# Attention and a cosine-gated MLP on one core: the weights' low-word bits taken by ScalarE from one byte, the word's shift folded into the join, and the gate's cosine as one sine

## The chip, the cores and the metric

The kernel runs on one core of one Trainium2 chip. The time is device microseconds of that core, from three executions of the kernel before: 662.24 us as their median, 661.46 and 663.5 us at the ends. The profile is of one more execution, taken by the hardware profiler.

## What is computed

Two stages. The first is attention over 4 batches, 8 heads, 768 positions and head size 64: each position sees its neighbours within 15 positions and, beside them, 24 summaries (the maximum of the keys and the mean of the values of each block of 32 positions). The second is an MLP on the 3072 resulting rows of 512 numbers, with a gate that multiplies by a cosine:

```python
x = np.ascontiguousarray(attn_out.transpose(0, 2, 1, 3)).reshape(B * S, H * D)
h = x @ w_in                 # 3072x512 @ 512x2048
g = h * np.cos(h)
return (g @ w_out).astype(np.float32)
```

The two weight matrices arrive as 64-bit floating-point numbers. The kernel has no 64-bit arithmetic, so it reads them as pairs of 32-bit integer words and puts a 32-bit number together from each pair.

## The kernel before

**Attention** is cut into 32 groups: 8 blocks of 384 rows, times 4 pairs of heads called a, b, c, d. A group's steps are transposes of queries and keys, score products, a maximum, a subtraction on POOL, an exponential on ACT, sums, a multiplication by their inverse on POOL, transposes of the weights of attention, and the product with the values, which leaves 128 columns of x, again as a high and a low part.

**The MLP** is cut into 128 *steps* s0 to s127, each of one block of 384 rows and one of 16 slices of 128 hidden units. Its products are done in a format with fewer mantissa bits, so every operand is split into a high part and a low part, and each product is three products. A step has *up* (12 matrix products, L714), then the gate, a chain on one tile t: *turns* (ACT, L724, h over 2 pi, rounded by the conversion to an integer), *residue* (DVE, L727, h minus 2 pi times the turns), *sine* (ACT, L732, of half the residue), *square* (ACT, L735, times 2), *gate* (DVE, L739, minus 1 and times h). Since cos h is 1 minus twice the squared sine of h/2, t then holds minus h cos h; the sign is put right when the result is taken from PSUM. Then *high_part* (a CAST to gh on ACT or DVE), *low_part* (gl), and 9 products with the second weights, L770: 6 with gh, 3 with gl. The steps run in the order block 0 slices 0 to 5, block 1 slices 0 to 15, block 0 slices 6 to 15, then the other blocks, 16 slices each.

**The weights' slices** w0 to w15 are converted in the first quarter of the program, each just ahead of the first step that uses it. A slice is 128x1024 pairs of words in one of the *late* buffers, and its steps are:

- *magnitude* (`ab`, ACT, L388): the high word read as a 32-bit float, made positive, into one of two *stage* buffers, `stage0` or `stage1`, each with room for one tile;
- *clamp* (`cl`, DVE or POOL, L393), in place;
- *shift* (`sh`, DVE, L399): the word shifted left by 3 and its two top bits masked off, from the stage buffer into two PSUM banks;
- *last_bits* (`lb`, DVE, L407), called the join from here on: the low word shifted right by 29, or-ed to it, in PSUM;
- *first_bits* (`fb`, DVE, L415): the high word's two top bits or-ed to it, from PSUM into a stage buffer;
- *high_part* and *low_part* (`hi`, L350 or L352; `lo`, L356): the slice's tile w.

**The order** is written out by hand. A string of tokens (`w3.sh.4.5` is slice 3's shift into banks 4 and 5; `s0.tu` is step 0's turns) is walked from the first to the last, each token issues its instructions, and every engine keeps its own instructions in that order. No scheduler moves them. Semaphores only make an engine wait where data or a buffer is not ready. So an instruction at the head of an engine's queue that waits holds back all that stand behind it there. The stage buffers add waits of their own: the magnitude of a slice can't write its stage buffer before the last reader of what lies there is done. In the kernel before that reader is the previous slice's shift; of a slice whose first_bits wrote into a stage buffer it is the low part.

The attention of blocks 0 and 1, the conversion of the slices, and the first MLP steps are interleaved in the first 95 us; after that most of the work is MLP steps, with the other blocks' attention between them.

Of the kernel before, what the change touches and what calls it, by code (L numbers as in the profile page):

```python
# [10 lines left out]
F32 = mybir.dt.float32  # L11
F32R = mybir.dt.float32r
I32 = mybir.dt.int32
AF = mybir.ActivationFunctionType
ALU = mybir.AluOpType
# [27 lines left out]
w8.sh.0.1 w3.hi.a b1.su a1.va.5 d1.z.0.v s1.tu c1.tp.0.7 w8.lb w3.lo.p a2.v d1.z.1.a c1.tp.1.3 s0.sq a2.tq.6 s1.re  # L43
c1.cp.1.a a1.xh.a s2.up.3 d1.mx s1.si c1.cp.0.a s0.ga d1.su w7.l w8.fb.0 s0.hi.a s1.sq c1.va.2 s0.lo.p w9.ab.1 s1.ga
w6.l s3.up.7 w8.hi.v s2.tu b2.q s1.hi.v d1.ex w9.cl.v s1.lo.p a1.xl s0.dh.0.1.4 s2.re w8.lo.p c1.xh.v s3.tu s0.dl
c1.xl s2.si s3.re s4.up.5 a2.cq.v v1_0.s.p d1.sm s2.sq s3.si s2.ga s1.dh w7.ab.0 d1.iv s2.hi.v d1.nm v1_1.l w9.sh.2.3
s1.dl s3.sq b1.ex s3.ga s2.lo.p d1.tp.0.6 w9.lb d1.tp.1.7 s2.dh w7.cl.p s4.tu b1.sm d1.cp.1.a s2.dl d1.cp.0.a s4.re
b1.iv s3.hi.a d1.va.7 w9.fb.1 b1.nm s4.si s5.up.6 w7.sh.2.3 s3.lo.p s4.sq w9.hi.v d1.xh.a s3.dh s4.ga s5.tu w9.lo.p
w10.ab.0 d1.xl s5.re s3.dl w7.lb s4.hi.a b1.tp.0.5 s5.si v1_1.s.p b1.tp.1.7 s4.dh b1.cp.1.a w7.fb.1 s5.sq b1.cp.0.a
s5.ga w7.hi.a b1.va.7 v1_2.l s4.lo.v w10.cl.v s4.dl s5.hi.a w7.lo.p b1.xh.a s5.dh b1.xl w10.sh.2.3 s6.up.5 v1_2.s.p  # L50
w6.ab.1 w10.lb s7.up.6 w10.fb.0 s6.tu s5.lo.p v1_3.l s6.re w12.l w6.cl.v s6.si s5.dl s7.tu w10.hi.v s8.up.7 s6.sq
s7.re w10.lo.p s5.ta.2.a s6.ga s7.si v1_3.s.v s7.sq s9.up.2 s5.ta.1.a s7.ga v1_4.l s6.hi.a w6.sh.4.5 s5.st.2 s5.ta.0.a
s6.lo.p b2.m s7.hi.a s10.up.3 s8.tu w6.lb s7.lo.p w12.ab.0 s8.re v1_4.s.p s11.up.6 w6.fb.1 s8.si s8.sq s9.tu s8.ga
v1_5.l w6.hi.a w12.cl.v s6.dh.4.5.7 w11.l s9.re w6.lo.p w12.sh.0.1 s9.si a2.m s6.dl s8.hi.a s7.dh s9.sq s5.st.1 s9.ga
s8.lo.p s5.st.0 w12.lb s7.dl s8.dh v1_5.s.p s10.tu s9.hi.a s10.re w12.fb.1 s10.si s8.dl s10.sq s12.up.2 v1_6.l
# [128 lines left out]
def tile_kernel(  # L184
# [20 lines left out]
    nc = tc.nc  # L205
# [156 lines left out]
    class Slice:  # L362
# [31 lines left out]

        def shift(self, *where):
            to = self.work_in(where)
            nc.vector.tensor_scalar(  # L399
                out=to, in0=self.u, scalar1=3, scalar2=0x3FFFFFFF,  # L400
# [557 lines left out]
```

## Time and profile before

| | |
|---|---|
| median of three executions | 662.24 us (661.46 to 663.5) |
| profiled execution, its span | 660.1 us |
| median less that span | 2.1 us |
| mean granted TensorE clock | 0.987 |
| HBM read, written | 53.72 MB, 15.73 MB |
| ACT table loads for the sine | 23, 29.5 us busy |

The profile counts, for each engine, the time in which an instruction ran. PE is the matrix engine's products and PEld its weight loads, which overlap them; DVE, ACT and POOL work on tiles; SP issues DMAs. A row of the groups' view gives line, engine, operation, output and input, shape and count, then the busy time in us and the mean of one in ns, then the engine's idle time just before these instructions and what ended most of it. A row of the timeline gives start and duration in us; a number after x is how many instructions the row joins, and square brackets hold the idle time ahead of it and the instruction or transfer that ended it. A row of the windows gives a stretch of the span and the busy time of each engine in it, then the granted clock, the DMA share and the rate.

### The profile page before, as it was taken

How to read it: one execution, taken by the hardware profiler on the slowest of the kernel's cores; microseconds unless marked ns; L12 is line 12 of the kernel's file. 1: busy time of each engine (PE TensorE's matmuls, PEld its weight loads, DVE VectorE, ACT ScalarE, POOL GpSimd, SP SyncE). 2: the span in 40 equal slices, each digit the busy share in tenths (PEclk: the TensorE clock that was granted, in tenths of full speed). 3: DMA queues.
4: the chain of work that ended last, by engine and by line, in shares of the span. 5: the costliest groups of instructions: out<-in, count | busy, mean ns of one | idle time of the engine just before them, and what ended most of it. 6: DMA issues, size and time to landing. Idle time of an engine off the chain costs nothing.

```text
span 660.1 us, 13282 instructions
## 1 busy us (share of the span) xinstructions
PE 632.6 (96%) x5141; PEld 560.2 (85%) x5141; DVE 449.7 (68%) x798; ACT 363.9 (55%) x640; POOL 221.8 (34%) x219
## 2 busy tenths in 40 slices
PE   6478999999999999999999999999999999999996
PEld 5256889989988998898898899889889989899985
DVE  4887999887855576668797777576876756433344
ACT  2656977776554485437477464356554645444342
POOL 4784896764430342301323411112330212010110
PEclk9869999999999999999999999999999999999999
DMA  9997906544243244525445433424364332000001
GB/s 224 259 271 203 276 15 223 169 109 71 55 122 85 91 124 132 127 59 114 111 107 135 147 98 97 114 43 85 115 163 104 92 94 70 5 1 17 16 17 48
DMA packets 167158, 72.68 MB, mean 110 GB/s; under 512 B 136824, under 2 KB 155832, under 8 KB 167096
## 3 DMA queue, kind: packets, MB, share of 16 engines
q1 hardware_dynamic: 167096, 71.84, 40.9%
q8 instruction: 40, 0.66, 0.4%
q14 instruction: 22, 0.18, 0.1%
HBM read 53.72 MB, written 15.73 MB: 105 GB/s over the span
## 4 chain that ended last, share of the span: by engine, by line
PE 86%; DMA 5%; SPq 3%; POOL 2%; DVE 1%; issue 1%; ACT 1%; DVEq 0%; POOLq 0%; ACTq 0%
PE banks L770 39%; PE banks L714 39%; PE banks L569 4%; PE banks L670 3%; DMA late<-in_moe_w_out_dram 3%; DMA late<-in_v_dram 1%; SPq L456 1%; POOL w L356 1%; DMA late<-in_q_dram 1%; POOL gl L356 1%; SPq L493 1%; POOL stage L393 0%; ACT stage L388 0%; PE banks L556 0%; DVE m L588 0%
## 5 line engine op out<-in xcount | busy, mean ns | idle before, releaser
L714 PE MATMUL banks<-xh,w 128*128 128x384 f32 x1024 | 272.1, 337 | 0.1
L770 PE MATMUL banks<-w,gh 128*128 128x512 f32 x768 | 198.1, 393 | 0.2 <-ACT gh L350 0.2
L714 PEld LDWEIGHTS banks<-xh,w 128*128 128x128 f32 x1024 | 185.9, 188 | 2.8 <-ACT pt L350 0.4
L714 PE MATMUL banks<-xl,w 128*128 128x384 f32 x512 | 171.4, 335 | 0.0
L770 PEld LDWEIGHTS banks<-w,gh 128*128 128x128 f32 x768 | 142.6, 188 | 29.0 <-ACT gh L350 0.5
L724 ACT ACTIVATE t<-banks 128x384 int32<-128x384 f32 x128 | 62.5, 489 | 133.6 <-DVE gl L356 54.9
L356 POOL TENSOR_TENSOR gl<-t,gh 128x384 fp32r<-128x384 f32 x55 | 56.6, 1029 | 221.4 <-ACT gh L350 86.0
L770 PE MATMUL banks<-w,gl 128*128 128x512 f32 x384 | 109.8, 394 | 0.1
L727 DVE SCALAR_TENSOR_TENSOR t<-t,banks 128x384 f32<-128x384 int32 x128 | 70.0, 548 | 56.9 <-ACT t L724 56.2
L732 ACT ACTIVATE t<-t 128x384 f32<-128x384 f32 x128 | 66.7, 523 | 66.3 <-DVE t L727 66.0
L714 PEld LDWEIGHTS banks<-xl,w 128*128 128x128 f32 x512 | 96.1, 188 | 1.6
L739 DVE SCALAR_TENSOR_TENSOR t<-t,banks 128x384 f32<-128x384 f32 x128 | 69.3, 546 | 41.2 <-ACT t L735 41.0
L770 PEld LDWEIGHTS banks<-w,gl 128*128 128x128 f32 x384 | 71.1, 188 | 14.6 <-DVE gl L356 0.2
L593 POOL TENSOR_TENSOR sc<-sc,m 128x720 f32<-128x720 f32 x28 | 40.1, 1431 | 129.2 <-DVE m L588 129.2
L735 ACT ACTIVATE t<-t 128x384 f32<-128x384 f32 x128 | 65.8, 521 | 2.1
L617 POOL TENSOR_TENSOR sc<-sc,r 128x720 f32<-128x720 f32 x28 | 39.5, 1411 | 51.4 <-DVE r L614 50.3
L350 ACT CAST gh<-t 128x384 fp32r<-128x384 f32 x68 | 34.7, 510 | 33.2 <-PE banks L770 16.5
L356 DVE TENSOR_TENSOR gl<-t,gh 128x384 fp32r<-128x384 f32 x73 | 41.7, 572 | 12.6 <-ACT gh L350 6.5
L356 POOL TENSOR_TENSOR w<-stage,w 128x1024 fp32r<-128x1024 f32 x15 | 36.2, 2416 | 10.0 <-ACT w L350 8.6
L352 DVE CAST gh<-t 128x384 fp32r<-128x384 f32 x60 | 23.2, 386 | 22.2 <-PE banks L770 20.4
L580 DVE SCALAR_TENSOR_TENSOR sc<-banks,mask 128x360 f32<-128x360 f32 x48 | 24.4, 524 | 19.2 <-PE banks L569 19.0
L569 PEld LDWEIGHTS banks<-kd,qd 64*64 64x64 f32 x1344 | 28.4, 135 | 9.4 <-issue 6.7
(102 smaller groups left out, 620.7 us busy)
## 6 DMA issues: line engine op xcount, KB each, us to landing
pd<-stage SPq DMA_DIRECT2D x22, 384.0 KB
late<-in_moe_w_in_dram SPq DMA_DIRECT2D x16, 512.0 KB
late<-in_moe_w_out_dram SPq DMA_DIRECT2D x16, 512.0 KB
pt<-pd SPq DMA_DIRECT2D x66, 96.0 KB
vn<-in_v_dram SPq DMA_DIRECT2D x52, 120.0 KB
out_dram<-stage SPq DMA_DIRECT2D x23, 256.0 KB
kn<-in_v_dram SPq DMA_DIRECT2D x24, 192.0 KB
qn<-in_q_dram SPq DMA_DIRECT2D x92, 48.0 KB
```

The costliest lines, as they stand in the source:

```text
L350: eng.copy(out=out, in_=in_)
L356: eng.tensor_tensor(out=lo, in0=src, in1=hi.bitcast(F32), op=ALU.subtract)
L569: nc.tensor.matmul(out=self.sp[hh][s * QT : (s + 1) * QT, c, lo : lo + n], lhsT=self.qd[rows, t * QT : (t + 1) * QT], rhs=self.kd[rows, ke ...
L593: nc.gpsimd.tensor_tensor(out=self.sc, in0=self.sc, in1=self.m.unsqueeze(2).broadcast_to([P, U, NK]), op=ALU.subtract)
L617: nc.gpsimd.tensor_tensor(out=self.sc, in0=self.sc, in1=self.r.unsqueeze(2).broadcast_to([P, U, NK]), op=ALU.mult)
L714: nc.tensor.matmul(out=self.h, lhsT=w_of(name, self.f)[:, c * P : (c + 1) * P], rhs=x_of(self.blk, part, c), start=n == 0, stop=n == last,)
L724: nc.scalar.activation(out=self.t.bitcast(I32), in_=self.h, func=AF.Copy, scale=1.0 / TWO_PI)
L727: nc.vector.scalar_tensor_tensor(out=self.t, in0=self.t.bitcast(I32), scalar=-TWO_PI, in1=self.h, op0=ALU.mult, op1=ALU.add)
L732: nc.scalar.activation(out=self.t, in_=self.t, func=AF.Sin, scale=0.5)
L735: nc.scalar.activation(out=self.t, in_=self.t, func=AF.Square, scale=math.sqrt(2.0))
L739: nc.vector.scalar_tensor_tensor(out=self.t, in0=self.t, scalar=-1.0, in1=self.h, op0=ALU.add, op1=ALU.mult)
L770: nc.tensor.matmul(out=self.acc[i], lhsT=g[:, i * P : (i + 1) * P], rhs=w_of(name, self.f), start=self.first and n == 0, stop=self.last an ...
```

## The change

Three edits in the code, and one in the order.

**The slices.** The magnitude now also multiplies by 2 to the power -48, and the clamp's two bounds are multiplied by the same, so that the word is small enough to be shifted by 3 with no mask. The shift step is gone. In its token's place, under the same name `sh` and with the same two PSUM banks, stands *top_bits*, on ACT: it reads one byte of eight (byte 3, the top one of the low word), multiplies by 1/32 and subtracts 15.5/32, and the conversion to an integer leaves the byte's three top bits. The join now shifts the word in the stage buffer left by 3 and ors the top bits in PSUM to it. first_bits keeps one bit of the high word where it kept two.

**The gate.** Turns adds a quarter (bias 0.25), sine takes minus the residue less pi/2, at scale 1 where it was 0.5, square is gone, and gate is one multiplication by h. t holds minus h cos h as before.

**The order.** The string of tokens is the same but for the 128 tokens `s0.sq` to `s127.sq`, which are left out; the slices' `sh` tokens stay where they were.

```diff
-    W_LO = struct.unpack("f", struct.pack("I", 896 << 20))[0]
-    W_HI = struct.unpack("f", struct.pack("I", (1151 << 20) - 1))[0]
+    DOWN = 2.0 ** -48
+    W_LO = struct.unpack("f", struct.pack("I", 896 << 20))[0] * DOWN
+    W_HI = struct.unpack("f", struct.pack("I", (1151 << 20) - 1))[0] * DOWN
...
-            nc.scalar.activation(out=self.u.bitcast(F32), in_=self.high.bitcast(F32), func=AF.Abs)
+            nc.scalar.activation(out=self.u.bitcast(F32), in_=self.high.bitcast(F32), func=AF.Abs, scale=DOWN)
...
-        def shift(self, *where):
-            to = self.work_in(where)
-            nc.vector.tensor_scalar(
-                out=to, in0=self.u, scalar1=3, scalar2=0x3FFFFFFF,
-                op0=ALU.logical_shift_left, op1=ALU.bitwise_and,
-            )
-            self.u = to
+        def top_bits(self, *where):
+            self.top = self.work_in(where)
+            byte = self.raw.bitcast(U8).rearrange("p (n b) -> p n b", b=8)[:, :, 3]
+            nc.scalar.activation(out=self.top, in_=byte, func=AF.Copy, scale=1.0 / 32, bias=-15.5 / 32)
 
         def last_bits(self, *where):
-            to = self.work_in(where)
+            to = self.work_in(where) if where else self.top
             nc.vector.scalar_tensor_tensor(
-                out=to, in0=self.low, scalar=29, in1=self.u,
-                op0=ALU.logical_shift_right, op1=ALU.bitwise_or,
+                out=to, in0=self.u, scalar=3, in1=self.top,
+                op0=ALU.logical_shift_left, op1=ALU.bitwise_or,
             )
             self.u = to
...
-                out=to, in0=self.high, scalar=-(1 << 30), in1=self.u,
+                out=to, in0=self.high, scalar=-(1 << 31), in1=self.u,
...
-            nc.scalar.activation(out=self.t.bitcast(I32), in_=self.h, func=AF.Copy, scale=1.0 / TWO_PI)
+            nc.scalar.activation(out=self.t.bitcast(I32), in_=self.h, func=AF.Copy, scale=1.0 / TWO_PI, bias=0.25)
...
-            nc.scalar.activation(out=self.t, in_=self.t, func=AF.Sin, scale=0.5)
-
-        def square(self):
-            nc.scalar.activation(out=self.t, in_=self.t, func=AF.Square, scale=math.sqrt(2.0))
+            nc.scalar.activation(out=self.t, in_=self.t, func=AF.Sin, scale=-1.0, bias=-0.5 * math.pi)
 
         def gate(self):
 
-            nc.vector.scalar_tensor_tensor(
-                out=self.t, in0=self.t, scalar=-1.0, in1=self.h, op0=ALU.add, op1=ALU.mult
-            )
+            nc.vector.tensor_tensor(out=self.t, in0=self.t, in1=self.h, op=ALU.mult)
...
-w8.sh.0.1 w3.hi.a b1.su a1.va.5 d1.z.0.v s1.tu c1.tp.0.7 w8.lb w3.lo.p a2.v d1.z.1.a c1.tp.1.3 s0.sq a2.tq.6 s1.re
-c1.cp.1.a a1.xh.a s2.up.3 d1.mx s1.si c1.cp.0.a s0.ga d1.su w7.l w8.fb.0 s0.hi.a s1.sq c1.va.2 s0.lo.p w9.ab.1 s1.ga
+w8.sh.0.1 w3.hi.a b1.su a1.va.5 d1.z.0.v s1.tu c1.tp.0.7 w8.lb w3.lo.p a2.v d1.z.1.a c1.tp.1.3 a2.tq.6 s1.re c1.cp.1.a
+a1.xh.a s2.up.3 d1.mx s1.si c1.cp.0.a s0.ga d1.su w7.l w8.fb.0 s0.hi.a c1.va.2 s0.lo.p w9.ab.1 s1.ga w6.l s3.up.7
```

The changed code is some lines shorter, so its line numbers differ: magnitude is L382 there, clamp L387, top bits L394, the join L398, first_bits L406, the copies L344 and L346, low parts and xl L350, up L705, turns L715, residue L718, sine L723, gate L727.

What this does to the engines' queues is shown at two places. Number endings such as `_586` are one use of a buffer; late_126, late_131, late_132 and late_127 hold the raw words of w3, w4, w7 and w10.

The first place is ACT's queue around the slices w3 and w4, before. `sc` and `late_130` are the scores of the groups a1 and c1, copied from PSUM in two halves; `stage_586` is w4's magnitude.

```order
L350 COPY sc<-banks 128x3x120 x2
L350 CAST xh_0_494<-banks 128x384
L508 ACTIVATE qd<-banks 128x384
L388 ACTIVATE stage_586<-late_131 128x1024
L350 CAST w_621<-stage_518 128x1024
L350 COPY late_130<-banks 128x3x120
L350 COPY pt<-banks 120x512
L350 COPY late_130<-banks 128x3x120
L350 COPY pt<-banks 120x256
L606 ACTIVATE sc<-sc 128x6x120
```

Nothing of a slice stands here but w4's magnitude and the high part of w5. The same stretch of ACT's queue now, from the first half of that `sc` copy on:

```order
L344 COPY sc<-banks 128x3x120
L394 ACTIVATE banks<-late_126 128x1024
L344 COPY sc<-banks 128x3x120
L344 CAST xh_0_494<-banks 128x384
L499 ACTIVATE qd<-banks 128x384
L382 ACTIVATE stage_586<-late_131 128x1024
L344 CAST w_621<-stage_518 128x1024
L344 COPY late_130<-banks 128x3x120
L344 COPY pt<-banks 120x512
L394 ACTIVATE banks<-late_131 128x1024
L344 COPY late_130<-banks 128x3x120
L344 COPY pt<-banks 120x256
```

Two rows are new, w3's top bits (from late_126) between the halves of one score copy, and w4's top bits (from late_131) between the first copy to pt and the second half of the other. They stand where the shifts stood in the program, but in the queue of another engine.

DVE's queue at the same place, before. L399 is the shift, L407 the join, L588 and L609 a group's maximum and sums, stage_505 w3's magnitude:

```order
L399 TENSOR_SCALAR banks<-stage_505 128x1024
L588 TENSOR_REDUCE m<-sc 128x6
L407 SCALAR_TENSOR_TENSOR banks<-late_126,banks 128x1024
L356 TENSOR_TENSOR xl_0_557<-banks,xh_0_494 128x384
L393 TENSOR_SCALAR stage_586<-stage_586 128x1024
L399 TENSOR_SCALAR banks<-stage_586 128x1024
L588 TENSOR_REDUCE m<-late_130 128x6
L407 SCALAR_TENSOR_TENSOR banks<-late_131,banks 128x1024
L609 TENSOR_REDUCE r<-sc 128x6
L356 TENSOR_TENSOR xl_0_487<-banks,xh_0_459 128x384
```

Each slice has a shift and, with one row between, a join. And now, where L398 is the join and L579 and L600 are the maximum and the sums:

```order
L579 TENSOR_REDUCE m<-sc 128x6
L398 SCALAR_TENSOR_TENSOR banks<-stage_505,banks 128x1024
L350 TENSOR_TENSOR xl_0_557<-banks,xh_0_494 128x384
L387 TENSOR_SCALAR stage_586<-stage_586 128x1024
L579 TENSOR_REDUCE m<-late_130 128x6
L398 SCALAR_TENSOR_TENSOR banks<-stage_586,banks 128x1024
L600 TENSOR_REDUCE r<-sc 128x6
L350 TENSOR_TENSOR xl_0_487<-banks,xh_0_459 128x384
```

Two rows are gone, the shifts of w3 and w4. The joins read stage_505 and stage_586, which they didn't before.

The second place is ACT's queue around the step s5 and the slices w7 and w10, before: s4's square, a copy of x, s5's turns, w10's magnitude (stage_1039, from late_127), s4's gh, s5's sine.

```order
L735 ACTIVATE t<-t 128x384
L350 CAST xh_1_911<-banks 128x384
L724 ACTIVATE t<-banks 128x384
L388 ACTIVATE stage_1039<-late_127 128x1024
L350 CAST gh<-t 128x384
L732 ACTIVATE t<-t 128x384
```

s4's gh stands right behind w10's magnitude. Now, with w7's top bits (from late_132) ahead of them, and w10's magnitude in stage_1034:

```order
L394 ACTIVATE banks<-late_132 128x1024
L344 CAST xh_1_909<-banks 128x384
L715 ACTIVATE t<-banks 128x384
L382 ACTIVATE stage_1034<-late_127 128x1024
L344 CAST gh<-t 128x384
L723 ACTIVATE t<-t 128x384
```

The square is gone and the top bits stand in the row ahead of the copy of x; the rest is as it was. DVE's queue there, before, from w7's shift (stage_949) to its first_bits; L727 is s5's residue and L407 w7's join:

```order
L399 TENSOR_SCALAR banks<-stage_949 128x1024
L352 CAST w_1026<-stage_1006 128x1024
L739 SCALAR_TENSOR_TENSOR t<-t,banks 128x384
L356 TENSOR_TENSOR xl_1_918<-banks,xh_1_911 128x384
L727 SCALAR_TENSOR_TENSOR t<-t,banks 128x384
L407 SCALAR_TENSOR_TENSOR banks<-late_132,banks 128x1024
L415 SCALAR_TENSOR_TENSOR stage_1068<-late_132,banks 128x1024
```

Shift and join of w7 are five rows apart. And now, with s5's residue in L718 and the join in L398, which reads stage_946. That is w7's magnitude, in the same buffer `stage0` that w10's magnitude then writes:

```order
L727 TENSOR_TENSOR t<-t,banks 128x384
L350 TENSOR_TENSOR xl_1_916<-banks,xh_1_909 128x384
L718 SCALAR_TENSOR_TENSOR t<-t,banks 128x384
L398 SCALAR_TENSOR_TENSOR banks<-stage_946,banks 128x1024
L406 SCALAR_TENSOR_TENSOR stage_1063<-late_132,banks 128x1024
```

The magnitude of w10 could start there as soon as w7's shift was done, three rows ahead of s5's residue; now the last reader of its buffer is w7's join, which stands behind that residue. PE, POOL and SP have the same instructions in the same order as before.

257 lines of the change are left out of this document (125 added, 132 removed).

## Prediction

> **What bounds the kernel now.** I read the engines' busy time first, then the windows by stage, then the groups, and last the timeline where PE is not full.
>
> ```profile
> PE 632.6 (96%) x5141; PEld 560.2 (85%) x5141; DVE 449.7 (68%) x798; ACT 363.9 (55%) x640; POOL 221.8 (34%) x219
> ...
> 40.00:60.00 20.00, 15.93 (x247) 11.76 (x244) 15.98 (x20) 12.14 (x24) 14.43 (x8) 0.87 0.71 181
> 60.00:80.00 20.00, 19.17 (x184) 16.54 (x183) 18.12 (x29) 17.93 (x29) 14.03 (x12) 1.00 1.06 317
> ...
> 100.00:600.00 500.00, 500.00 (x4015) 449.53 (x4014) 345.93 (x642) 278.20 (x487) 144.66 (x131) 1.00 0.39 101
> 600.00:660.10 60.10, 55.12 (x272) 48.96 (x271) 21.90 (x44) 21.68 (x46) 6.07 (x6) 1.00 0.06 22
> ```
>
> The first line is each engine's sum, the others are windows (length, then busy time of PE, PEld, DVE, ACT, POOL). From 100 to 600 us PE is busy all of 500.00 us, ACT only 278.20 and DVE 345.93. There the kernel is bound by the products: whatever ACT and DVE save in that stretch is idle time of theirs. The end can move only where PE is not full, in the first 95 us. There ACT and DVE are loaded: 17.93 and 18.12 of 20 us from 60 to 80. From then on PE has no gaps to take a delay back, so what it loses before 95 us reaches the end undiminished; the 5.0 us in which it is not busy in the last window go with the last outputs, whose steps the change leaves alone.
>
> **What goes: squares and shifts.** The groups' rows (line, engine, operation, tiles, count, then busy us and mean ns, then idle before and what ended it):
>
> ```profile
> L735 ACT ACTIVATE t<-t 128x384 f32<-128x384 f32 x128 | 65.8, 521 | 2.1
> ...
> L399 DVE TENSOR_SCALAR banks<-stage 128x1024 int32<-128x1024 int32 x16 | 19.6, 1222 | 1.8 <-POOL stage L393 1.0 <-ACT late L350 0.6
> ...
> L388 ACT ACTIVATE stage<-late 128x1024 f32<-128x1024 f32 x16 | 18.4, 1151 | 11.5 <-DMA late<-in_moe_w_out_dram 7.1 <-DVE banks L399 2.3 <-POOL w L356 2.1
> ...
> L350 ACT CAST w<-stage 128x1024 fp32r<-128x1024 f32 x13 | 13.6, 1044 | 2.3 <-DVE stage L415 2.2
> ```
>
> 128 squares of 521 ns are 65.8 us of ACT, 16 shifts of 1222 ns are 19.6 us of DVE. Both look large. But nearly all of the squares run while PE is at 500 of 500, so I cost their loss there at nothing: what is late next is still PE itself. The new bias of turns and sine, and the gate as one multiplication, I take at the old durations; a tenth of a us more or less on each would vanish in the same idle time. The 16 shifts stand in the first 150 us and matter only for what is said below.
>
> **What comes: top bits on ACT.** No row shows ACT reading bytes, or writing 1024 numbers to PSUM. The nearest rows have the same engine and shape: the CAST of a whole tile at 1.04 us, and the magnitude, which also reads one word of every eight bytes, at 1.15. I take 1.10 and keep 1.0 to 1.2 as ends; a slower reading of bytes is a rival. In a chain of ACT instructions it adds 1.0, as the rows below overlap by 0.1 (a magnitude at 50.58 of 1.17 us would end at 51.75, by the rows the next CAST starts at 51.64 us).
>
> The Trainium skill, ScalarE: Activation LUTs, section What ACT_TABLE_LOAD costs, gives 186 ns and 0.833 ns per element for an ACTIVATE with immediate scale and bias, which is 1.04 us here as an estimate. The CAST's row agrees, the strided magnitude's 1.15 does not; by the page the sum below would be +2.4.
>
> **First place: 37 to 70 us.** Timeline rows (start, duration, engine, line; in brackets the idle time ahead and what ended it), the attention of two blocks with w5, w3 and w4:
>
> ```profile
> 40.86 0.48 ACT L350 CAST xh<-banks 128x384 fp32r<-128x384 f32 x1 [0.43 <-PE banks L670]
> ...
> 42.39 1.14 ACT L388 ACTIVATE stage<-late 128x1024 f32<-128x1024 f32 x1 [1.05 <-DMA late<-in_moe_w_out_dram]
> ...
> 44.49 0.49 ACT L508 ACTIVATE qd<-banks 128x384 f32<-128x384 f32 x1 [0.97 <-PE banks L502]
> ...
> 48.29 0.82 ACT L350 COPY sc<-banks 128x360 f32<-128x360 f32 x2 [1.48 <-PE banks L569]
> ...
> 49.14 0.90 DVE L588 TENSOR_REDUCE m<-sc 128x6 f32<-128x720 f32 x1
> ...
> 49.96 1.22 DVE L407 SCALAR_TENSOR_TENSOR banks<-late,banks 128x1024 int32<-128x1024 int32 x1
> ...
> 50.58 1.17 ACT L388 ACTIVATE stage<-late 128x1024 f32<-128x1024 f32 x1
> ...
> 51.64 1.03 ACT L350 CAST w<-stage 128x1024 fp32r<-128x1024 f32 x1
> ...
> 53.41 0.47 ACT L350 COPY late<-banks 128x360 f32<-128x360 f32 x1
> ...
> 53.76 0.40 ACT L350 COPY pt<-banks 120x256 f32<-120x256 f32 x1
> ...
> 54.20 0.89 DVE L588 TENSOR_REDUCE m<-late 128x6 f32<-128x720 f32 x1
> ...
> 55.01 1.22 DVE L407 SCALAR_TENSOR_TENSOR banks<-late,banks 128x1024 int32<-128x1024 int32 x1
> ...
> 56.14 0.90 DVE L609 TENSOR_REDUCE r<-sc 128x6 f32<-128x726 f32 x1
> ...
> 56.71 0.92 PE L670 MATMUL banks<-pt,vn 120*64 120x64 f32 x24 [2.27 <-DMA vn<-in_v_dram]
> 56.96 2.38 POOL L356 TENSOR_TENSOR w<-stage,w 128x1024 fp32r<-128x1024 f32 x1
> ...
> 58.18 0.56 DVE L356 TENSOR_TENSOR xl<-banks,xh 128x384 fp32r<-128x384 f32 x1 [1.14 <-ACT xh L350]
> ...
> 58.88 0.43 PE L714 MATMUL banks<-xh,w 128*128 128x384 f32 x1
> ...
> 59.30 1.39 POOL L617 TENSOR_TENSOR sc<-sc,r 128x720 f32<-128x720 f32 x1
> ...
> 61.06 0.60 PE L626 MATMUL banks<-ident,sc 128*120 128x128 f32 x4
> ...
> 68.33 0.43 PE L626 MATMUL banks<-ident,late 128*120 128x128 f32 x2 [0.47 <-DVE late L352]
> ...
> 68.99 0.55 PE L502 MATMUL banks<-ident,qn 128*128 128x128 f32 x3 [0.22 <-ACT late L350]
> ```
>
> The new wait: a magnitude can write its stage buffer only after the previous slice's join, and the join only starts after that slice's top bits, which stand in ACT's queue ahead of the magnitude. ACT waits for DVE, which waited for ACT; copies that PE needs stand behind.
>
> It starts with w3's magnitude (42.39, released by a DMA). w5's top bits follow the xh of 40.86: 41.24 to 42.34, w5's join to 43.6, the magnitude to 44.8, and qd would start at 44.66, +0.2. Three slices' top bits stand earlier in ACT's queue, 3.0 us, most of them covered by its waits for DMAs; of what they leave I carry +0.5 (between 0 and 0.8). So qd is at +0.7.
>
> The score copies of 48.29 then start at 48.99, w3's top bits run from 49.35 to 50.45 between them, and the second copy ends at 50.8. The maximum takes DVE from 50.83, and w3's join, 0.82 later as in the rows, runs from 51.65 to 52.87. w4's magnitude comes at 52.9 instead of 50.58: **+2.3**.
>
> w4's top bits add 1.0: the copies of 53.41 and 53.76 come at +3.3, so PE's L670 starts at 57.5, not 56.71. On DVE the maximum starts at 57.2, w4's join runs from 58.0 to 59.2, the sums to 60.05, xl to 60.5: PE's first up starts at 60.55, not 58.88, +1.7. On POOL the subtraction of 1.39 starts behind that maximum, at 58.1, the low part of 2.38 ends at 61.85, L617 at 63.25: PE's L626 starts there, not at 61.06, **+2.2**.
>
> At 68.33 and 68.99 PE waited 0.47 and 0.22 us for copies. The first copy stood behind w8's shift on DVE, which is gone, so up to 0.7 comes back. I take 0.5: +1.7 behind this place, with ends 1.4 and 2.2.
>
> **Second place: 87 to 93 us.** Rows of s5's gate beside w7's join and w10's magnitude:
>
> ```profile
> 86.98 0.33 PE L714 MATMUL banks<-xh,w 128*128 128x384 f32 x1
> ...
> 88.27 0.49 ACT L724 ACTIVATE t<-banks 128x384 int32<-128x384 f32 x1 [1.45 <-POOL gl L356]
> ...
> 88.66 1.18 ACT L388 ACTIVATE stage<-late 128x1024 f32<-128x1024 f32 x1
> 88.80 0.55 DVE L727 SCALAR_TENSOR_TENSOR t<-t,banks 128x384 f32<-128x384 int32 x1 [0.50 <-ACT t L724]
> ...
> 89.27 1.22 DVE L407 SCALAR_TENSOR_TENSOR banks<-late,banks 128x1024 int32<-128x1024 int32 x1
> 89.70 0.54 ACT L350 CAST gh<-t 128x384 fp32r<-128x384 f32 x1
> ...
> 90.29 1.66 PE L770 MATMUL banks<-w,gh 128*128 128x512 f32 x6 [0.22 <-ACT gh L350]
> ```
>
> Before, w10's magnitude ran straight behind the turns, gh followed, and PE waited 0.22 us for gh. Now gh stands behind a magnitude that waits for w7's join, which stands behind s5's residue: turns to residue 0.53, to the join 0.47, the join 1.22, the magnitude 1.04 to the start of gh, gh 0.54, 3.8 us in all with 0.03 between engines. Turns start with the end of s5's up, 87.31 + 1.7 + 0.05 = 89.06, so PE's L770 starts at 92.9 instead of 90.29: **+2.6**, the 1.7 carried in and 0.9 more. With nothing carried in, turns would still start at 88.27 and PE at 92.1, +1.8. That is the floor of this place, whatever the first one does.
>
> **The sum.** Behind 95 us I find no row where PE waits for a slice, so the end moves by +2.6 us: the span from 660.1 to 662.7. The runs' median is 2.1 us above the span; I leave that, and get 662.24 + 2.6 = **664.8 us**. With 1.4 to 2.2 carried in the sum is 2.3 to 3.1; with top bits of 1.0 to 1.2, which count three times in a row (w5, w3, w4), another 0.3 either way; with 0 to 0.8 for the carry into 44.49, another -0.5 or +0.3. The forecast's own range is 663.6 to 666.2.
>
> **Rivals.** *Bytes are slow.* If ACT takes 1.6 to 2.2 us for the top bits, three in a row add 1.5 to 3.3 to the sum: 666.3 to 668.1. Against it: strided words cost only 0.11 over the CAST. Chance 0.12.
>
> *Hidden.* PE's L670 of 56.71 waited 2.27 us for a DMA, and the head's transfers take 0.71 and more of the DMA engines, so the first place may be late for other reasons; other short waits of PE that return may also pay for the second place. 661.2 to 663.4, chance 0.22. Against it: the floor of +1.8.
>
> *Not slower, by DVE's relief.* Two waits of PE hang on short queues, 0.47 and 0.22 in the first place, and 0.22 in the second. Without shifts of 1.22 us DVE could end them: 0.9 less, 661.3. It decides if joins end before ACT comes to the next magnitude: 50.58 for w4. But even with no delay the join of w3 would follow the maximum of 49.14 and end at 51.2 at best. Chance 0.08.
>
> *The gates were the limit.* One group's row of weight loads, and one piece of the chain of waits:
>
> ```profile
> L770 PEld LDWEIGHTS banks<-w,gh 128*128 128x128 f32 x768 | 142.6, 188 | 29.0 <-ACT gh L350 0.5
> ...
> 149.69 2.09 PE banks L770 x9
> ```
>
> If the 29.0 us of idle weight loads were waits for gates, a gate shorter by a square could give up to all of it: 633.2. But only 0.5 of them ended with gh; 29.0 over 768 is 38 ns each, and a product takes 2.09/9 = 232 ns against 188 for its load, which leaves 44. Chance 0.02. The Trainium skill, Perfetto Trace Analysis, section Identifying the Most-Contended Engine, speaks for this rival: it judges TensorE's headroom by the weight loads' busy share and not by the products', and that share is 85% here.
>
> **How the numbers follow.** The forecast has 0.56; with the rivals' 0.12, 0.22, 0.08 and 0.02 that is all. About 0.3% is what a measurement of this kernel can tell from no change, 2.0 us: slower begins at 664.23, faster at 660.25. Of the forecast's 0.56 some 0.47 lies above 664.23; with slow bytes and a trace of the hidden case that is 0.60. Faster has the gates' 0.02 and the lowest tails of two rivals, 0.06; the rest, 0.34, is the same. The range leaves out DVE's relief, the gates, the lower fifth of the hidden case and the upper third of slow bytes, in sum 0.19: 661.8 to 667.6.
>
> **What would show it.** In the changed kernel's profile: the top bits' group at 16 times 1.10 us; magnitudes with idle time ahead that ends with the join on DVE (before, 2.3 us with the shift); PE's first up near 60.5, L626 near 63, and a wait of some 1.7 us ahead of the L770 behind s5's turns; from 100 to 600 us PE at 500 again. If PE's first up is where it was, the first place is wrong; if PE waits behind 100 us, the sum is incomplete; if the top bits take 2 us, the size is.

## The result, and the profile after

The changed kernel took 665.9 us (median of five runs, 664.82 to 666.59), the kernel before 663.21 us over five runs of the same session: a ratio of 1.0055, 95% interval 1.004 to 1.007, so it is slower by 2.7 to 4.6 us. That ratio is the one on record; the quotient of the two medians, 1.0041, lies at the lower end of its interval. The profiled execution has a span of 663.5 us, 3.4 more than the 660.1 before. A second series of six runs, beside the experiments, gave 666.37 us, ratio 1.0072 (1.0047 to 1.0096). The forecast was 664.8 in a range of 661.8 to 667.6.

The windows of the changed kernel (length, busy time of PE, PEld, DVE, ACT, POOL, granted clock, DMA share, rate):

```profile
60.00:80.00 20.00, 18.46 (x180) 16.14 (x181) 17.77 (x27) 17.29 (x27) 16.30 (x10) 1.00 0.84 252
80.00:100.00 20.00, 17.84 (x129) 14.94 (x128) 15.42 (x22) 16.74 (x25) 17.80 (x17) 1.00 0.20 57
100.00:600.00 500.00, 500.00 (x4014) 449.37 (x4013) 338.68 (x636) 233.78 (x384) 145.60 (x133) 1.00 0.39 102
```

From 100 to 600 us ACT is busy 233.78 us where it was 278.20, and PE is at 500.00 as before: 44 us less work for ACT there, and nothing for the end. Before 100 us PE has lost time: 18.46 us busy for 19.17 in the first of these windows, 17.84 for 19.73 in the second.

The groups of the new and the touched instructions:

```profile
L756 PE MATMUL banks<-w,gh 128*128 128x512 f32 x768 | 198.1, 393 | 1.9 <-ACT gh L344 1.9
...
L398 DVE SCALAR_TENSOR_TENSOR banks<-stage,banks 128x1024 int32<-128x1024 int32 x16 | 19.6, 1224 | 9.3 <-ACT banks L394 9.3
...
L382 ACT ACTIVATE stage<-late 128x1024 f32<-128x1024 f32 x16 | 18.2, 1140 | 12.6 <-DVE banks L398 7.9 <-DMA late<-in_moe_w_out_dram 4.1 <-POOL w L350 0.5
...
L394 ACT ACTIVATE banks<-late 128x1024 int32<-128x1024 uint8 x16 | 17.6, 1098 | 0.0
```

Read the idle columns together: DVE sat 9.3 us ahead of joins for ACT's top bits, ACT sat 7.9 us ahead of magnitudes for DVE's joins (it was 2.3, for shifts), and PE waited 1.9 us for a gh from ACT (0.2 before). The top bits cost 1.098 us each.

The first place in the timeline (start, duration, engine, line; in brackets the idle time ahead and what ended it):

```profile
46.34 0.47 ACT L499 ACTIVATE qd<-banks 128x384 f32<-128x384 f32 x1
...
47.67 1.09 PE L560 MATMUL banks<-kd,qd 64*64 64x96 f32 x48
...
48.82 0.46 ACT L344 COPY sc<-banks 128x360 f32<-128x360 f32 x1 [0.19 <-PE banks L560]
...
49.18 1.14 ACT L394 ACTIVATE banks<-late 128x1024 int32<-128x1024 uint8 x1
...
50.74 0.90 DVE L579 TENSOR_REDUCE m<-sc 128x6 f32<-128x720 f32 x1 [1.74 <-ACT sc L344]
...
51.56 1.22 DVE L398 SCALAR_TENSOR_TENSOR banks<-stage,banks 128x1024 int32<-128x1024 int32 x1
...
52.81 1.15 ACT L382 ACTIVATE stage<-late 128x1024 f32<-128x1024 f32 x1 [1.34 <-DVE banks L398]
...
55.63 1.10 ACT L394 ACTIVATE banks<-late 128x1024 int32<-128x1024 uint8 x1
...
57.17 0.92 PE L661 MATMUL banks<-pt,vn 120*64 120x64 f32 x24 [0.50 <-ACT late L344]
...
59.91 0.55 DVE L350 TENSOR_TENSOR xl<-banks,xh 128x384 fp32r<-128x384 f32 x1
...
60.51 0.44 PE L705 MATMUL banks<-xh,w 128*128 128x384 f32 x1 [0.93 <-DVE xl L350]
...
62.27 1.39 POOL L608 TENSOR_TENSOR sc<-sc,r 128x720 f32<-128x720 f32 x1
...
63.72 0.65 PE L617 MATMUL banks<-ident,sc 128*120 128x128 f32 x4 [0.85 <-POOL sc L608]
...
71.25 0.44 PE L705 MATMUL banks<-xh,w 128*128 128x384 f32 x1
```

w4's magnitude starts at 52.81 (50.58 before) when w3's join is done, and PE's first up at 60.51 (58.88). By the first product of s2's up, at 71.25, PE is 1.58 us behind the kernel before, where that product starts at 69.67.

The second place:

```profile
88.49 1.47 POOL L350 TENSOR_TENSOR gl<-t,gh 128x384 fp32r<-128x384 f32 x1
...
88.89 0.33 PE L705 MATMUL banks<-xh,w 128*128 128x384 f32 x1
...
89.99 0.49 ACT L715 ACTIVATE t<-banks 128x384 int32<-128x384 f32 x1 [0.36 <-POOL gl L350]
...
90.52 0.55 DVE L718 SCALAR_TENSOR_TENSOR t<-t,banks 128x384 f32<-128x384 int32 x1 [0.29 <-ACT t L715]
90.99 1.22 DVE L398 SCALAR_TENSOR_TENSOR banks<-stage,banks 128x1024 int32<-128x1024 int32 x1
...
92.25 1.13 ACT L382 ACTIVATE stage<-late 128x1024 f32<-128x1024 f32 x1 [1.76 <-DVE banks L398]
...
93.28 0.50 ACT L344 CAST gh<-t 128x384 fp32r<-128x384 f32 x1
...
93.83 1.65 PE L756 MATMUL banks<-w,gh 128*128 128x512 f32 x6 [1.86 <-ACT gh L344]
```

The chain is the one forecast: turns, residue, join, magnitude, gh. PE waits 1.86 us and starts at 93.83 instead of 90.29, 3.54 late; the span's end is 3.4 late.

### The profile page after: what moved, and what is told of

Same layout as the page of the kernel before. It is cut to its first block, busy times and chain, and to the rows that moved or that the text cites. A ratio compares the mean times of both kernels' runs of the same rounds, so it can differ in the third digit from the quotient of the medians.

```text
span 663.5 us, 13159 instructions
## 1 busy us (share of the span) xinstructions
PE 631.4 (95%) x5141; PEld 559.7 (84%) x5141; DVE 433.6 (65%) x782; ACT 320.7 (48%) x528; POOL 221.3 (33%) x219
## 4 chain that ended last, share of the span: by engine, by line
PE 85%; ACT 0%; DVEq 0%; DVE 0%; issue 0%
PE banks L756 39%; PE banks L705 39%; PE banks L560 4%; PE banks L661 3%; PE banks L617 0%; ACT stage L382 0%; PE banks L506 0%; DVEq L939 0%; DVE last L794 0%; ACT gh L344 0%; ACT last L792 0%
## 5 line engine op out<-in xcount | busy, mean ns | idle before, releaser
L705 PE MATMUL banks<-xh,w 128*128 128x384 f32 x1024 | 272.0, 337 | 0.9 <-DVE xl L350 0.9
L705 PEld LDWEIGHTS banks<-xh,w 128*128 128x128 f32 x1024 | 185.9, 188 | 3.6 <-DVE xl L350 1.2
L705 PE MATMUL banks<-xl,w 128*128 128x384 f32 x512 | 171.4, 335 | 0.0
L715 ACT ACTIVATE t<-banks 128x384 int32<-128x384 f32 x128 | 62.4, 489 | 162.0 <-DVE gl L350 60.7
L350 POOL TENSOR_TENSOR gl<-t,gh 128x384 fp32r<-128x384 f32 x55 | 57.4, 1043 | 225.6 <-PE banks L756 108.7
L718 DVE SCALAR_TENSOR_TENSOR t<-t,banks 128x384 f32<-128x384 int32 x128 | 70.0, 548 | 70.8 <-ACT t L715 69.8
L723 ACT ACTIVATE t<-t 128x384 f32<-128x384 f32 x128 | 66.5, 524 | 73.4 <-DVE t L718 73.1
L705 PEld LDWEIGHTS banks<-xl,w 128*128 128x128 f32 x512 | 96.1, 188 | 1.6
L727 DVE TENSOR_TENSOR t<-t,banks 128x384 f32<-128x384 f32 x128 | 69.1, 544 | 15.1 <-ACT t L723 14.1
L344 ACT CAST gh<-t 128x384 fp32r<-128x384 f32 x68 | 34.7, 511 | 43.4 <-PE banks L756 22.3
L350 DVE TENSOR_TENSOR gl<-t,gh 128x384 fp32r<-128x384 f32 x73 | 41.6, 571 | 18.0 <-PE banks L756 9.8
L346 DVE CAST gh<-t 128x384 fp32r<-128x384 f32 x60 | 23.9, 399 | 28.5 <-PE banks L756 26.4
L350 POOL TENSOR_TENSOR w<-stage,w 128x1024 fp32r<-128x1024 f32 x15 | 36.3, 2420 | 13.4 <-ACT w L344 11.1
L661 PEld LDWEIGHTS banks<-pt,vn 120*64 120x64 f32 x624 | 21.0, 141 | 12.9 <-ACT pt L344 7.1
```

The costliest lines, as they stand in the source:

```text
L344: eng.copy(out=out, in_=in_)
L350: eng.tensor_tensor(out=lo, in0=src, in1=hi.bitcast(F32), op=ALU.subtract)
L661: nc.tensor.matmul(out=self.xps[rows, t * QT : (t + 1) * QT], lhsT=self.vn[:, t, rows], rhs=self.pt[2 * c + hh][s], start=True, stop=True,)
L705: nc.tensor.matmul(out=self.h, lhsT=w_of(name, self.f)[:, c * P : (c + 1) * P], rhs=x_of(self.blk, part, c), start=n == 0, stop=n == last,)
L715: nc.scalar.activation(out=self.t.bitcast(I32), in_=self.h, func=AF.Copy, scale=1.0 / TWO_PI, bias=0.25)
L718: nc.vector.scalar_tensor_tensor(out=self.t, in0=self.t.bitcast(I32), scalar=-TWO_PI, in1=self.h, op0=ALU.mult, op1=ALU.add)
```

## The experiments

Theory A: the loss is made in these two places, by the loop of waits between ACT (top bits, then the next magnitude) and DVE (the join), and the gate's part gains and costs nothing. The rivals stand in the expectations. Each time is a median beside runs of the kernel before on the same chip; the difference in us is the ratio less one, times that kernel's median. The ratios on record are not the quotients of the two medians; by the medians alone a difference comes out up to 1 us larger or smaller, so less than that is not told apart here.

### The gate's part alone

```diff
-            nc.scalar.activation(out=self.t, in_=self.t, func=AF.Sin, scale=0.5)
+            nc.scalar.activation(out=self.t, in_=self.t, func=AF.Sin, scale=-1.0, bias=-0.5 * math.pi)
...
-        def square(self):
```

> The kernel before with the gate's part of the change alone: bias in the turns, one sine, no square, one multiplication; the slices' decoding with its shift on DVE is as before. Theory A (the 2.7 us come from the decoding in the first 95 us; the squares were hidden behind PE): within 1 us of the kernel before, PE's first up of s0 at 58.9 +- 0.6 us of the profile and the products behind s4's gh at about 90, no wait above 0.5 us there. Rival B (the gate's new form costs the time): +2 to +3 us. Rival C (shorter gates pay a little in the head): -1 to -2 us.

662.74 us against 662.17, ratio 1.0009 (0.9993 to 1.0024): +0.6 us, no difference. 128 squares of 0.52 us were worth nothing by themselves, and the new gate costs nothing. The profiled execution was the slowest of the twelve and late from early on (w1's magnitude, which waits for a DMA, at 23.26 us for 21.74; its first up at 63.74), so its places can't be compared in time; but PE's group behind the gates has no wait:

```profile
L757 PE MATMUL banks<-w,gh 128*128 128x512 f32 x768 | 198.1, 393 | 0.0
```

### The decoding's part alone

```diff
+            nc.scalar.activation(out=self.t, in_=self.t, func=AF.Sin, scale=0.5)
+
+        def square(self):
+            nc.scalar.activation(out=self.t, in_=self.t, func=AF.Square, scale=math.sqrt(2.0))
...
-            nc.vector.tensor_tensor(out=self.t, in0=self.t, in1=self.h, op=ALU.mult)
+            nc.vector.scalar_tensor_tensor(
+                out=self.t, in0=self.t, scalar=-1.0, in1=self.h, op0=ALU.add, op1=ALU.mult
+            )
```

> The changed kernel with the old gate (sine of half, square, gate in two operations) and the old order with its squares; only the slices' decoding is changed. Theory A: at least the whole loss, +2.5 to +4 us over the kernel before, the squares of s0 to s4 adding up to 0.5 us each time one stands ahead of a copy for PE; the wait of PE ahead of the products with s4's gh at 1.5 us or more. Rival B (gate): within 1 us of the kernel before.

668.71 us against 662.17, ratio 1.0086 (1.0063 to 1.0108): +5.7 us, over the range expected. The sign is A's, and so is the wait of PE. By their middle values the two parts don't add up: the gate's part is worth nothing on the kernel before, but 1 to 2 us here, by the two series of the changed kernel. The intervals overlap, though (+4.2 to +7.2 us here, +3.1 to +6.4 in the changed kernel's second series), so this is not shown. The squares of s0 to s4 in a queue of ACT that is now late are a candidate for a part of it only: w4's magnitude, ahead of every square, comes at 53.58 in this profile and at 52.81 in the changed kernel's, so 0.77 us of its lateness were there before. The row of the second place:

```profile
95.20 2.18 PE L769 MATMUL banks<-w,gh 128*128 128x512 f32 x6 [1.95 <-ACT gh L352]
```

PE starts there 4.9 us behind the kernel before (90.29), and the six products take 2.18 us where they took 1.66: that belongs to the clock, in the last section.

### No top bits: the buffer's wait without the work on ACT

```diff
-            nc.scalar.activation(out=self.top, in_=byte, func=AF.Copy, scale=1.0 / 32, bias=-15.5 / 32)
...
-            nc.vector.scalar_tensor_tensor(
-                out=to, in0=self.u, scalar=3, in1=self.top,
-                op0=ALU.logical_shift_left, op1=ALU.bitwise_or,
+            nc.vector.tensor_scalar(
+                out=to, in0=self.u, scalar1=3, scalar2=0x7FFFFFFF,
+                op0=ALU.logical_shift_left, op1=ALU.bitwise_and,
             )
```

> The changed kernel without the top bits: ACT has nothing in their place, and the join on DVE only shifts the word, so the low word's three bits are left out of the weights. The magnitude still waits for the previous slice's join. It tells the buffer's wait from the work on ACT. Theory A1 (the wait for the join alone, with its place behind the residue, makes most of the second place): the wait of PE for s4's gh stays at 1.3 to 2 us, the first place keeps +0.5 (w4's magnitude 0.6 later), and the kernel is +1.5 to +2.5 us over the kernel before. Rival A2 (the 1.1 us on ACT per slice are what costs): within 0.7 us of the kernel before, no such wait.

664.29 us against 662.17, ratio 1.0029 (1.0016 to 1.0042): +1.9 us. The first place is whole again: PE's first up starts at 58.20 with no wait, where A1 expected 0.5 us to be left. The second isn't:

```profile
58.20 0.44 PE L703 MATMUL banks<-xh,w 128*128 128x384 f32 x1
...
90.17 1.15 ACT L382 ACTIVATE stage<-late 128x1024 f32<-128x1024 f32 x1 [1.76 <-DVE banks L396]
...
91.76 2.65 PE L754 MATMUL banks<-w,gh 128*128 128x512 f32 x6 [2.20 <-ACT gh L344]
```

So both halves of the question have an answer, one for each place: at the second the buffer's later release alone makes the wait, with no top bits at all; at the first it takes the top bits in ACT's queue.

### w10's magnitude behind s5's sine

```diff
-s5.tu w9.lo.p w10.ab.0 d1.xl s5.re s3.dl w7.lb s4.hi.a b1.tp.0.5 s5.si v1_1.s.p
+s5.tu w9.lo.p d1.xl s5.re s3.dl w7.lb s4.hi.a b1.tp.0.5 s5.si w10.ab.0 v1_1.s.p
```

> The changed kernel with one token moved: w10's magnitude stands behind s5's sine in ACT's queue instead of behind s5's turns, so that s4's gh no longer stands behind a magnitude that waits. Theory A: the wait of 1.86 us ahead of the products with s4's gh goes, PE is 1.5 to 2.0 us earlier from 95 us on, and the time is +0.5 to +1.3 us over the kernel before (about 1.7 less than the changed kernel). Rival D (the lateness is only handed on: w10, or s5's own gate, is late next): no gain over the changed kernel, another wait of 1 us or more for w10's tile or for s5's gh before 110 us.

665.23 us against 662.17, ratio 1.0045 (1.0027 to 1.0062): +3.0 us, more than A expected. In the profile, which is that of the fastest of its nine runs (663.36 us), the wait for gh is gone, PE starts at 91.01; but the waiting magnitude now stands ahead of copies to pt, and PE waits for these:

```profile
91.01 1.64 PE L756 MATMUL banks<-w,gh 128*128 128x512 f32 x6
91.51 1.14 ACT L382 ACTIVATE stage<-late 128x1024 f32<-128x1024 f32 x1 [0.61 <-DVE banks L398]
...
93.44 0.92 PE L661 MATMUL banks<-pt,late 120*64 120x64 f32 x24 [0.79 <-ACT pt L344]
```

A part of the lateness is handed on, as rival D had it, by a wait of 0.79 us where D expected 1 or more. With an interval of 2.3 us the times can't say how much of the gain is left; the move of the waiting instruction is the weaker cure.

### The changed kernel again, and the top bits twice

```diff
             nc.scalar.activation(out=self.top, in_=byte, func=AF.Copy, scale=1.0 / 32, bias=-15.5 / 32)
+            nc.scalar.activation(out=self.top, in_=byte, func=AF.Copy, scale=1.0 / 32, bias=-15.5 / 32)
```

> The changed kernel itself, unaltered, on the same chip as the next three, to compare them with it: +2 to +4 us over the kernel before.

> The changed kernel with every slice's top bits issued twice in a row, the same numbers into the same banks: 1.1 us more of ACT for each slice. Theory A (the top bits stand in the chain magnitude - top bits - join - next magnitude, one slice after the other): w5, w3 and w4 alone add 3.0 us in the first place, and what the waits for DMAs covered before (w1, w0, w2) is covered no more: +5 to +12 us over the changed kernel. Rival E (the loss is the buffer's wait, a fixed cost, and ACT has room): less than +1.5 us over the changed kernel.

666.37 and 680.08 us against 661.92, ratios 1.0072 (1.0047 to 1.0096) and 1.0279 (1.0261 to 1.0297). The changed kernel is at +4.8 us, above the 2 to 4 expected of it. A second helping of 16 times 1.1 us costs 13.7 us, above the 5 to 12 expected. Of 17.5 us put into ACT's queue more than three quarters come out at the end. The rows of w3 and w4 in the kernel with two show the loop, now with PE late by 10 us behind it:

```profile
54.84 1.13 ACT L394 ACTIVATE banks<-late 128x1024 int32<-128x1024 uint8 x1
56.00 1.09 ACT L395 ACTIVATE banks<-late 128x1024 int32<-128x1024 uint8 x1
...
58.33 1.22 DVE L399 SCALAR_TENSOR_TENSOR banks<-stage,banks 128x1024 int32<-128x1024 int32 x1
...
59.58 1.15 ACT L382 ACTIVATE stage<-late 128x1024 f32<-128x1024 f32 x1 [1.34 <-DVE banks L399]
```

Rival E falls. Why the first helping cost so much less is open. ACT's waits for DMAs ahead of magnitudes went from 7.1 us before to 4.1 in the changed kernel, so they covered a part of it; but they were not used up then, with two helpings 6.1 us are left. PE's clock is one more difference: the granted clock from 40 to 60 and from 60 to 80 us is 0.73 and 0.83 with two helpings, 0.88 and 1.00 with one.

### An early join, and top bits moved: a cure that fell

```diff
-            nc.scalar.activation(out=self.top, in_=byte, func=AF.Copy, scale=1.0 / 32, bias=-15.5 / 32)
+            nc.scalar.activation(out=self.low, in_=byte, func=AF.Copy, scale=1.0 / 32, bias=-15.5 / 32)
...
-                out=to, in0=self.u, scalar=3, in1=self.top,
+                out=to, in0=self.u, scalar=3, in1=self.low,
...
-d0.va.3 b0.iv w3.sh.4.5 b0.nm a1.z.0.a b1.m c1.ms.7.2 d0.xh.a a1.mx c1.cq.a d1.q w4.ab.0 c1.sc w3.lb a1.su
+d0.va.3 b0.iv w3.lb.4.5 b0.nm a1.z.0.a b1.m c1.ms.7.2 d0.xh.a a1.mx c1.cq.a d1.q w4.ab.0 w4.tp c1.sc a1.su
```

`w4.tp` is w4's top bits. In the second kernel three such tokens stand later still, as its expectation says.

> The changed kernel with the top bits written over the low words themselves, right behind each magnitude, and the join in the place that the shift had in DVE's queue, into the same banks. The work on ACT is the same as in the changed kernel, but the stage buffer is free as early as before. Theory A (the wait through the join costs most): PE's first up of s0 is back within 0.6 us of 58.9, PE's wait for s4's gh is at most 1.2 us, and the time is +0.5 to +1.5 us over the kernel before, 1.5 us or more below the changed kernel. Rival F (17.6 us more of ACT in the first 150 us is what costs, wherever it stands): within 0.7 us of the changed kernel.

> The same as the kernel with the early join, and three slices' top bits moved behind copies that PE waits for: w10's behind s4's gh and two copies to pt, w7's behind s3's gh, w8's behind a copy to pt with its join ahead of its first_bits. Theory A: nothing is left on PE's path, within 0.8 us of the kernel before; the square and the shift gained nothing, so it is not faster by more than 0.7 us either. Rival F: within 0.7 us of the changed kernel. Rival G (DVE's 19.6 us of shifts were worth something once nothing waits): -1 us or better against the kernel before.

671.94 and 674.44 us against 661.92, ratios 1.0147 (1.0131 to 1.0164) and 1.0188 (1.0167 to 1.0209): far slower than any theory had it. The edit had a side that none of them counted: the join's two inputs now both lie in SBUF, where one was in PSUM. The group and the timeline of the first of the two kernels:

```profile
L397 DVE SCALAR_TENSOR_TENSOR banks<-stage,late 128x1024 int32<-128x1024 int32 x16 | 28.6, 1789 | 3.5 <-POOL stage L387 2.0 <-DMA late<-in_v_dram 0.6 <-issue 0.5
```

```profile
50.72 1.40 POOL L607 TENSOR_TENSOR sc<-sc,r 128x720 f32<-128x720 f32 x1
50.79 2.42 DVE L397 SCALAR_TENSOR_TENSOR banks<-stage,late 128x1024 int32<-128x1024 int32 x1 [1.29 <-POOL stage L387]
...
56.73 1.23 DVE L397 SCALAR_TENSOR_TENSOR banks<-stage,late 128x1024 int32<-128x1024 int32 x1 [0.61 <-DMA late<-in_v_dram]
```

Alone it takes 1.23 us as before; begun just behind a POOL instruction it takes 2.42, about the rest of that one and its own time. Of the 16 joins in this profile eight took 1.60 to 3.31 us, each begun while POOL was at work, and the other eight 1.22 or 1.23. The mean went from 1224 to 1789 ns. These two kernels therefore say nothing on A or F.

### The same idea with the top bits left in PSUM: tokens moved only

```diff
-w9.hi.v d1.xh.a s3.dh s4.ga s5.tu w9.lo.p w10.ab.0 d1.xl s5.re s3.dl w7.lb s4.hi.a
+w9.hi.v d1.xh.a s3.dh w7.lb s4.ga s5.tu w9.lo.p w10.ab.0 d1.xl s5.re s3.dl s4.hi.a
```

That is the second place's move; the next are the first place's, of w3, w4 and w8:

```diff
-a1.z.1.a d0.va.3 b0.iv w3.sh.4.5 b0.nm a1.z.0.a b1.m c1.ms.7.2 d0.xh.a a1.mx c1.cq.a
-d1.q w4.ab.0 c1.sc w3.lb a1.su
+w3.sh.4.5 a1.z.1.a d0.va.3 b0.iv b0.nm a1.z.0.a b1.m c1.ms.7.2 d0.xh.a w3.lb a1.mx c1.cq.a
+d1.q w4.ab.0 c1.sc a1.su
...
-b0.cp.0.a w4.sh.6.7 c1.z.1.a b1.ms.3.0 b0.cp.1.a v1_0.l c1.mx a1.ex w8.l w4.lb c1.su b0.va.2 b1.sc a1.sm
+b0.cp.0.a c1.z.1.a b1.ms.3.0 b0.cp.1.a v1_0.l c1.mx a1.ex w4.sh.6.7 w8.l c1.su b0.va.2 b1.sc a1.sm w4.lb
...
-w8.sh.0.1 w3.hi.a
+w3.hi.a
...
-c1.cp.1.a a1.xh.a
+c1.cp.1.a w8.sh.0.1 a1.xh.a
...
-w7.l w8.fb.0
+w7.l w8.lb w8.fb.0
```

> The changed kernel with one token moved: w7's join stands ahead of s4's gate in DVE's queue, so ahead of s5's residue, and w10's magnitude, right behind s5's turns in ACT's queue as before, need not wait for it. Instructions and buffers are the changed kernel's. Theory A: PE's wait of 1.9 us ahead of the products with s4's gh is 0.6 us or less; the time is 1 to 2 us below the changed kernel, +1.5 to +2.5 us over the kernel before. Rival F (17.6 us more of ACT cost, wherever they stand): within 0.7 us of the changed kernel.

> The changed kernel with the first place's tokens moved and the second left: w3's top bits ahead of both halves of a1's score copy and its join ahead of a1's maximum; w4's top bits behind the exponential and its join behind the sums; w8's top bits behind a copy to pt and its join ahead of its first_bits. Theory A: PE's first up of s0 at 58.9 +- 0.6 us, PE's wait for s4's gh still there at 0.8 to 2 us; +0.5 to +1.7 us over the kernel before. Rival F: within 0.7 us of the changed kernel.

> Both sets of moves together; every slice still has its 1.1 us of top bits on ACT, with the same instructions, buffers and banks as the changed kernel. Theory A: nothing of the loss is left, within 0.8 us of the kernel before, and not faster by more than 0.7 us, since the squares and shifts were hidden. Rival F: within 0.7 us of the changed kernel. Rival G (the shorter work of ACT and DVE is worth something once the waits are gone): -1 us or better against the kernel before.

Against 662.74 us: the second place alone 664.65, ratio 1.003 (1.0013 to 1.0047), +2.0 us, as A expected; the first alone 664.9, ratio 1.0042 (1.0025 to 1.006), +2.8 us, more than the 0.5 to 1.7 that A expected; both 663.82, ratio 1.0022 (1.0008 to 1.0035), +1.5 us. The instructions, buffers and banks are the changed kernel's, which had +3.6 and +4.8 us in its two series; it was not run again beside these. In the timeline of the kernel with w7's join moved:

```profile
90.03 1.18 ACT L382 ACTIVATE stage<-late 128x1024 f32<-128x1024 f32 x1
...
91.67 1.66 PE L756 MATMUL banks<-w,gh 128*128 128x512 f32 x6 [0.24 <-ACT gh L344]
```

of the kernel with the first place's moves alone:

```profile
90.62 1.16 ACT L382 ACTIVATE stage<-late 128x1024 f32<-128x1024 f32 x1 [1.76 <-DVE banks L398]
...
92.23 1.66 PE L756 MATMUL banks<-w,gh 128*128 128x512 f32 x6 [2.23 <-ACT gh L344]
```

and of the kernel with both:

```profile
91.28 1.16 ACT L382 ACTIVATE stage<-late 128x1024 f32<-128x1024 f32 x1
...
92.89 1.66 PE L756 MATMUL banks<-w,gh 128*128 128x512 f32 x6 [0.38 <-ACT gh L344]
```

The magnitude has a wait of 1.76 us ahead exactly where w7's join was left in its place, and PE's wait for gh follows it: 0.24, 2.23, 0.38 us. With the first place's moves alone PE's first up starts at 59.01, 0.13 us behind the kernel before. Rival F falls: the same 17.6 us on ACT cost +0.5 to +2.3 us when they stand elsewhere, by the interval, and +2.7 to +4.6 or +3.1 to +6.4 in the changed kernel's two series. Rival G falls too, nothing is faster than the kernel before. But +1.5 us with both moves is more than the 0.8 that A allowed, though the interval reaches below it; by the medians it is +1.1.

### Without the first four slices' top bits

```diff
+            if self.f in (0, 1, 2, 5):
+                return
             byte = self.raw.bitcast(U8).rearrange("p (n b) -> p n b", b=8)[:, :, 3]
```

> The kernel with both sets of moves, and no top bits for w1, w0, w2 and w5, the four slices decoded before 45 us, whose tokens were not moved: their join only shifts, so three bits of their low words are left out. If what was left over the kernel before (+1.1 us) comes from these four slices' top bits, the time is within 0.6 us of the kernel before. If it comes from elsewhere (the moved tokens themselves, or the other twelve slices), it stays at +0.8 to +1.6 us.

663.01 us against 662.56, ratio 1.0008 (0.9987 to 1.0028): +0.5 us, within what was expected if the rest comes from the four slices decoded before 45 us. The interval reaches from -0.9 to +1.9 us and holds the 1.5 as well, so where the rest comes from stays open.

## Why the prediction came out as it did

**Right: what goes gains nothing.** PE is at 500.00 of 500 us with and without the squares, and the gate's part alone makes no difference (ratio 1.0009).

**Right: the price of the top bits and their path at the first place.** 1.098 us was measured where 1.10 was taken. w4's magnitude came 2.23 us late (2.3 forecast), PE's first up at 60.51 (60.55), L617 at 63.72 (63.25), and 1.58 us were left behind it (1.7). The order of joins and maxima is that of the sum.

**Luck in part: how close these numbers are.** The term carried in from the three earlier slices was mis-sized. It was +0.5, between 0 and 0.8; the trace has the xh ahead of w5's top bits at 42.52 for 40.86, 1.66 late, and qd at 46.34, 1.85 late where the sum had 0.7. The score copies came at 48.82 all the same, 0.53 late (0.7 in the sum), because PE's work between them and qd was shorter. Before, the score products were:

```profile
46.36 1.86 PE L569 MATMUL banks<-kd,qd 64*64 64x96 f32 x48
```

In the changed kernel they took 1.09 us. The granted clock from 46 to 48 us was 0.50 before and 1.00 after, for which the sum has no term. Likewise L617 was 2.66 late for 2.2 in the sum, and the copies behind it gave back 1.08 for 0.5. And in the five profiles of kernels with the same instructions up to PE's first up it starts anywhere from 59.78 to 61.28 us, so an agreement to 0.04 is chance.

**Right in mechanism, mis-sized: the second place.** Forecast were the 1.7 carried in and 0.9 more, 2.6 in all; the trace has 3.54. The term that failed is the start of s5's turns: the sum let them start with the end of s5's up, at 89.06, on the view that POOL's gl, which ended ahead of turns at 88.27 before, was on time. But POOL's work hangs on the same late first place: the clamp and the multiplication ahead of gl started at 83.56 and 87.14 instead of 81.83 and 85.42, gl at 88.49 instead of 86.77, 1.72 late, and turns at 89.99. That is 0.7 us of the 0.9 missing; another 0.2 is the up itself, whose last product came 1.91 late (88.89 for 86.98) where 1.7 was taken. From there to PE's products it took 3.84 us, with 3.8 forecast. A floor worked out for a punctual engine was used beside a carry that makes that engine late too. The floor itself held: with the first place's moves alone turns start at 88.37 (88.27 in the prediction) and the products at 92.23 (92.1).

**The rivals.** Slow bytes, the hidden case, DVE's relief and gates as the limit are all out: the top bits took 1.098 us, both waits appear in the rows, the shorter waits of PE behind the first place gave back 1.08 us of 2.66 and not the whole, and PE gained nothing from shorter gates. In the kernel with both sets of moves the loss is below half, which is as near to the hidden case as the runs came.

**The profile and the median.** The forecast went by one profiled execution. The profile moved by 3.4 us and the medians by 2.7, and in the second series by 4.5; the runs of one kernel spread over 3 us and more, part of it by the clock, below. That the 2.7 lies beside the forecast's 2.6 is therefore luck too: the trace in which the steps can be read moved by more. The forecast's own range was also added up too wide: its terms give +1.5 to +3.7, so 663.7 to 665.9 us, for the 663.6 to 666.2 stated.

## What to carry to other kernels

Work given to an idle engine is free only at a place where nothing urgent stands behind it in that engine's queue: 17.6 us of top bits on an engine with 55% busy time cost 3 to 5 us, and less than half of that after a few tokens were moved. When an operation takes over the reading of a buffer from an earlier one, ask who waits for that buffer to be free, and what stands between the new reader and its place in the queue. And when a delay is carried forward, carry it into every engine that feeds the next place, not into one.

## What was not expected of the hardware

**PE's clock fell behind waits of about 2 us, in some executions.** Windows around the second place, of the changed kernel's first profile:

```profile
92.00:94.00 2.00, 0.17 (x1) 0.17 (x2) 1.44 (x2) 1.75 (x3) 1.76 (x5) 1.00 0.00 0
94.00:96.00 2.00, 2.00 (x26) 1.47 (x28) 1.63 (x3) 2.00 (x5) 0.34 (x2) 1.00 0.16 57
```

and of its second, with the same wait of 1.86 us:

```profile
92.00:94.00 2.00, 0.24 (x3) 0.00 (x0) 1.69 (x2) 1.50 (x3) 1.84 (x4) 1.00 0.00 0
94.00:96.00 2.00, 1.90 (x5) 1.52 (x6) 1.50 (x3) 2.00 (x5) 0.50 (x2) 0.55 0.11 38
96.00:98.00 2.00, 2.00 (x27) 1.33 (x25) 0.13 (x1) 0.57 (x2) 1.77 (x1) 0.60 0.17 60
```

The granted clock (third number from the end) stayed at 1.00 in one and fell to 0.55 and 0.60 in the other, whose six products with gh took 2.86 us instead of 1.65; at the products behind them PE was then 5.0 us late instead of 3.5. Of five profiles with a wait of 1.86 to 2.23 us there, three show it: from the start of these six products to that of the next six with gh it takes 4.72 to 4.75 us in the three, 3.23 and 3.25 in the others. So a wait of this length costs itself and, in some runs, 1.5 us on top. The Trainium skill, TensorE: Matmul & The Clock Gate, section What's actually happening, has the array fall to half speed after an idle window of about 3.4 us; here waits of 1.86 us were enough, though not each time.

**DVE with two inputs in SBUF waits for POOL.** The join's 1.23 and 2.42 us above. The Trainium skill, SBUF — State Buffer, section SBUF: two separate sides, states it: an instruction of VectorE with two SBUF inputs and one of GpSimd that reads SBUF lock each other out for the whole instruction. The rows agree, 2.42 us being a little less than the 1.33 left of POOL's and 1.22 of its own together; with one input in PSUM the joins of the kernels before and after stayed at 1.21 to 1.23 us under the same POOL work.
